# QKV product of tiles 6 to 15 as seven products of halves, second LayerNorm by algebra, W1 cast at the end of the stage

## The chip, the cores and the metric

One Trainium2 chip, one of its cores. The time is device microseconds of one execution, and lower is better. The kernel before takes 1277.43 us, the median of three runs (1275.66 to 1277.49). A profiled execution stands beside them; all shares and durations below are from it. Engines: PE (TensorE, products), ACT (ScalarE), DVE (VectorE), POOL (GpSimd), SP (which issues most DMAs).

## The reference

x has 2048 tokens of 576 features. Three things are added up, all on a normalized x.

```python
xn = _layernorm(x)
# A: sliding, dilated attention, 32 heads of 18
qkv = xn @ wqkv                                  # 576 x 1728
# each token sees itself and 7 earlier ones, 2 apart
a = softmax(q . k * 18**-0.5) . v @ wo
# B: a mixer
h = gelu(_layernorm(xn) @ w1)                    # 576 x 576
hs = shift_by_quarters(h) @ w2                   # +1, -1, +2, -2 tokens
x1 = xn + hs
b = x1 + gelu(_layernorm(x1) @ w3) @ w4          # 576 x 4608 x 576
out = x + a + b
```

The change touches `qkv = xn @ wqkv` and what is made beside it: xn, `_layernorm(xn)` and W1's cast.

## The kernel before, in words

Everything is float32, but products run on operands rounded to `fp32r`. To keep precision each operand is split into a rounded part "hi" (a cast on ACT) and the rest "lo" (a subtraction on DVE), and hi x hi, hi x lo and lo x hi are added up. With 576 = 4 x 128 + 64 features that makes 14 matmuls for one block of output, listed in `PAIRS`; the odd 64 features stand once as hi and once as lo in one slot.

A tile is 128 tokens; there are 16, and Y keeps all of them in SBUF. The order of the work on each engine is that of the Python code (`manual_schedule`): each engine and the DMA queue of SP take their instructions strictly in that order, and wait at semaphores. The stages are: QKV (to 194.9 us), the mixer with W1 and W2, the first part of the MLP plainly (with attention on DVE in between), the rest of the MLP by products of halves (`HALVES`, seven matmuls for a block of 288 features), and Wo.

The QKV stage, on which the change bears:

- `load_x`, `stats` and `norm_x` bring a tile, take its mean and variance (two BN_STATS, one aggregate, one addition on DVE, a power on POOL) and normalize it into Y. A second `stats(Y, 1, t)` takes them again for the second LayerNorm.
- `prep_x` (`transposes`, L137 to L149) turns a tile on PE (four transposes of 128 x 128 and every second tile a fifth for two tiles' odd features), casts hi on ACT (L142, L145) and takes lo on DVE (L146, L149).
- wqkv comes in five groups of columns (`COLS`: three of 288, two of 432) and is split once into WQ by `split_cg`.
- Tiles 0 to 3 take each group of columns as it comes (`q_cg`, L314, 14 matmuls, a copy L317 out of PSUM, a spill to DRAM). Tiles 4 to 15 take two halves of 864 columns each (`q_half` with `mm_tok`, L215: 28 matmuls of 432 columns, one copy L324, one spill).
- Beside them, tiles 0 to 15 are normalized again on DVE (`z_turn`), turned in 32 x 32 blocks (L161, L162) and put into DRAM, from where the mixer reads them by feature (`get`, `split_x`).
- `split_w1` casts W1 beside tiles 5 and 6, early in the stage; its tiles have a place of their own.

Of the kernel before, what the change touches and what calls it, by code (L numbers as in the profile page):

```python
# [17 lines left out]
NT = S // 128  # L18
# [39 lines left out]
def fused_block(ctx, tc, x, wqkv, wo, w1, w2, w3, w4, out):  # L58
# [46 lines left out]
    ztail = {}  # L105

    def tail_half(t):
        if t % 2 == 0:
            ztail[t // 2] = qpool.tile([128, 128], F32, name="ztail", bufs=2)
        return ztail[t // 2][:, t % 2 * 64:t % 2 * 64 + 64]  # L110

    def pair_tail(src, xts, t):
        return (src, [(xts, (t % 4 - 1) * 128), (xts, (t % 4) * 128)]) if t % 2 else None

# [16 lines left out]

    def transposes(src, tail, xt, col):
        ps = psb.tile([128, 2, 512], F32, name="ps", tag="b")
        p0 = ps[:, 0, :].rearrange("p (k c) -> p k c", k=4)
        p1 = ps[:, 1, :128]
        for k in range(4):
            pe.transpose(p0[:, k, :], src[:, k * 128:(k + 1) * 128], ident)  # L137
        rows = tail[0].shape[1] if tail else 0
        if tail:
            pe.transpose(p1[:rows], tail[0], ident)  # L140
        c = slice(col, col + 128)
        act.copy(xt[:, 0:4, c], p0)  # L142
        for i in range(rows // 64):
            xtt, ct = tail[1][i]
            act.copy(xtt[0:64, 4, ct:ct + 128], p1[64 * i:64 * i + 64])  # L145
        dve.tensor_tensor(xt[:, 5:9, c], p0, xt[:, 0:4, c].bitcast(F32), op=ALU.subtract)  # L146
        for i in range(rows // 64):
            xtt, ct = tail[1][i]
            dve.tensor_tensor(xtt[64:128, 4, ct:ct + 128], p1[64 * i:64 * i + 64],  # L149
                              xtt[0:64, 4, ct:ct + 128].bitcast(F32), op=ALU.subtract)  # L150

# [64 lines left out]
    w1p = tc.tile_pool(name="w1p", bufs=1, side="right", reuse_waits="tile")  # L218
    w1pool = w1p.__enter__()
    W1 = w1pool.tile([128, 10, 512], F32R, name="W1")  # L220
    W1R = w1pool.tile([128, 5, 128], F32R, name="W1R")
    room(w1pool)

    def z_turn(t):
        z = w1pool.tile([128, D], F32, name="z", bufs=1)
        norm(z, Y[:, t, :], 1, t)
        turn(z, t % 4)

    qp = tc.tile_pool(name="qp", bufs=1, reuse_waits="tile")
    qpool = qp.__enter__()  # L230
    WQ = qpool.tile([128, 10, 3 * D], F32R, name="WQ")
    xtile = {}
    xring = {}
    CG = 432
    COLS = [(0, 288), (288, 288), (576, 288), (864, 432), (1296, 432)]

    def load_x(t):
        xtile[t] = qpool.tile([128, D], F32, name="xin", bufs=3)
        sp.dma_start(xtile[t], xf[t * 128:(t + 1) * 128, :])

    def norm_x(t):
        norm(Y[:, t, :], xtile[t], 0, t)
        if t >= 4:
            dve.tensor_copy(tail_half(t), Y[:, t, 512:])
# [6 lines left out]
    def prep_x(t):  # L251
        xt = ring_block(("q", t // 4))
        if t < 4:
            tail = (Y[:, t, 512:], [(xt, t * 128)])
        else:
            tail = pair_tail(ztail[t // 2], xt, t)
        transposes(Y[:, t, :], tail, xt, (t % 4) * 128)
# [3 lines left out]
    def load_cg(cg, pieces):  # L261
        c, n = COLS[cg]
        r = qraw[cg] = qpool.tile([128, 5, n], F32, name="raw", bufs=2)
        if pieces:
            main_rows(r[:, 0:2, :], wqkv, c, n, 0, 2)
            main_rows(r[:, 2:4, :], wqkv, c, n, 2, 4)
        else:
            main_rows(r[:, 0:4, :], wqkv, c, n)
        dup_tail(r[:, 4, :], wqkv, c, n)
# [4 lines left out]

    load_x(0)
    load_x(1)
    load_cg(0, True)
    load_x(2)
    load_cg(1, False)
    load_x(3)  # L280
# [1189 lines left out]
```

## Time and profile before

| | |
|---|---|
| runs | 1277.49, 1275.66, 1277.43 us |
| profiled execution | 1279.68 us, its span from the first to the last instruction 1277.8 us |
| granted PE clock over the span | 0.998 |
| 0 to 8 us | PE 6.55 busy, DVE 3.75, ACT 3.19 |
| 8 to 20 us | PE 10.43 busy, DVE 9.31, ACT 5.21 |
| 195 to 254 us (mixer, W1) | PE 59.00 busy, DVE 34.79, ACT 36.05 |
| DMA over the span | 223.25 MB in 203800 packets, mean 175 GB/s |
| qkvd<-stg, x24 | 432 KB each, 3.9 us from issue to landing |

A row of the timeline reads: start, duration of the merged rows, engine, line, operation, out<-in, shape, count, and in brackets the idle time ahead of it with its releaser. In a group row the count is followed by the busy time, the mean ns of one, and the idle time ahead.

### The profile page before, as it was taken

To read this page: it belongs to the slowest core of one execution; us is meant where nothing else is said; L and a number is where in the kernel's file an instruction comes from. 1 tells how busy PE (TensorE), PEld (TensorE's weight loads), DVE (VectorE), ACT (ScalarE), POOL (GpSimd) and SP (SyncE) were. 2 spreads that over 40 slices of the span, in tenths; PEclk is the share of its full clock that TensorE was granted. 3 is DMA by queue.
4 is the path that set the end of the run, shared out by engine and by line. 5 is a ranking of instruction groups with operands and counts; after the bars stand their busy time and mean duration, and the time that the engine had idled before them with its cause. 6 is when DMAs were issued, how large, how long until landed. Compare 5 with 4: busy or idle time off the path is not lost.

```text
span 1277.8 us, 19971 instructions
## 1 busy us (share of the span) xinstructions
PE 1261.6 (99%) x7510; PEld 1155.8 (90%) x7510; DVE 900.3 (70%) x1203; ACT 722.2 (57%) x1155; POOL 253.0 (20%) x366
## 2 busy tenths in 40 slices
PE   9999999999999999999999999999999999999999
PEld 8999998899889999999889999998889898898898
DVE  6455533777648999998649998989899884464341
ACT  3332225525645545455777777776667776677730
POOL 2011100021122121212122232232122222222200
PEclk9999999999999999999999999999999999999999
DMA  7646774346897977769669889888958769899982
GB/s 206 154 123 141 165 173 145 85 119 200 192 239 167 231 146 158 151 141 243 119 131 213 197 175 219 183 162 209 259 84 197 146 116 189 183 213 216 259 256 84
DMA packets 203800, 223.25 MB, mean 175 GB/s; under 512 B 79528, under 2 KB 139528, under 8 KB 203576
## 3 DMA queue, kind: packets, MB, share of 16 engines
q1 hardware_dynamic: 170952, 155.18, 42.6%
q0 software_dynamic: 32752, 66.80, 32.6%
q8 instruction: 59, 0.97, 0.3%
q14 instruction: 37, 0.30, 0.1%
HBM read 124.47 MB, written 107.87 MB: 182 GB/s over the span
## 4 chain that ended last, share of the span: by engine, by line
PE 63%; DMA 3%; ACT 2%; DVE 2%; issue 1%; SPq 0%; DVEq 0%; ACTq 0%
PE ps L868 30%; PE cc L1130 19%; PE p L832 10%; PE ps L215 4%; DMA w3st<-in_B_w_dram 1%; DMA xt<-xn 1%; DVE w3st L965 1%; DMA x1n<-td1T 0%; DVE xt L597 0%; SPq L1178 0%; DMA Y<-od 0%; PE p L1437 0%; ACT Y L873 0%; ACT xt L927 0%; DVE w3a L976 0%
## 5 line engine op out<-in xcount | busy, mean ns | idle before, releaser
L868 PEld LDWEIGHTS ps<-w,c 128*128 128x128 f32 x3456 | 475.2, 188 | 22.5 <-ACT Y L873 3.2
L868 PE MATMUL ps<-w,c 128*128 128x288 f32 x3456 | 486.1, 294 | 6.2 <-ACT Y L873 2.1
L874 POOL DMA_DIRECT2D yd<-Y x154 | 138.4, 902 | 394.5 <-ACT Y L873 323.9
L826 DVE TENSOR_TENSOR c<-Y,c 128x512 fp32r<-128x512 f32 x144 | 98.8, 687 | 88.9 <-ACT Y L815 87.4
L873 ACT COPY Y<-ps 128x576 f32<-128x576 f32 x154 | 98.1, 637 | 75.2 <-PE ps L868 61.7
L215 PE MATMUL ps<-WQ,xt 128*128 128x432 f32 x672 | 134.8, 360 | 0.0
L215 PEld LDWEIGHTS ps<-WQ,xt 128*128 128x128 f32 x672 | 125.6, 188 | 5.7
L1130 PE MATMUL cc<-xt,w3s 128*128 128x512 f32 (+1 forms) x504 | 128.4, 394 | 1.0 <-DVE Y L1140 1.0
L1130 PEld LDWEIGHTS cc<-xt,w3s 128*128 128x128 f32 (+1 forms) x504 | 92.6, 189 | 19.5 <-DVE Y L1140 1.4
L876 ACT COPY Y<-ps 128x576 f32<-128x576 f32 x92 | 59.0, 641 | 65.6 <-PE ps L868 64.2
L1130 PE MATMUL cc<-x1n,w3a 128*128 128x512 f32 (+1 forms) x336 | 87.2, 399 | 1.4 <-ACT cc L1333 1.4
L746 DVE TENSOR_TENSOR po<-q,k 128x1152 f32<-128x1152 f32 (+1 forms) x48 | 84.3, 1756 | 0.8
L749 DVE TENSOR_REDUCE L<-po 128x64 f32<-128x1152 f32 (+1 forms) x48 | 84.1, 1751 | 0.8
L122 POOL TENSOR_TENSOR rs<-rs,mhalf 128x1 f32<-128x1 f32 x48 | 30.9, 645 | 260.1 <-DVE rs L121 147.7
L324 ACT COPY stg<-ps 128x864 f32<-128x864 f32 x24 | 21.2, 882 | 102.7 <-PE ps L215 60.4
L814 ACT ACTIVATE c<-p 128x512 fp32r<-128x512 f32 x48 | 28.7, 599 | 85.7 <-PE p L832 85.7
L722 DVE TENSOR_TENSOR po<-v,L 128x1152 f32<-128x1152 f32 x56 | 75.4, 1354 | 0.9
L1140 DVE TENSOR_TENSOR Y<-cc,Y 128x512 f32<-128x512 f32 x49 | 33.7, 688 | 59.9 <-ACT Y L1136 55.1
L1130 PEld LDWEIGHTS cc<-x1n,w3a 128*128 128x128 f32 (+1 forms) x336 | 61.1, 190 | 13.1 <-ACT cc L1333 1.9
L726 DVE TENSOR_TENSOR po<-po 128x1152 f32<-128x1152 f32 x49 | 66.4, 1355 | 0.9
L849 ACT COPY ps<-Y 128x576 f32<-128x576 f32 x92 | 59.4, 645 | 4.4 <-DVE Y L879 2.4
L215 PE MATMUL ps<-W,h 128*128 128x288 f32 x384 | 53.5, 295 | 0.0
(192 smaller groups left out, 1954.5 us busy)
## 6 DMA issues: line engine op xcount, KB each, us to landing
yd<-Y POOLq DMA_DIRECT2D x156, 288.0 KB, 5.8
Y<-in_B_w_dram SPq DMA_DIRECT2D x29, 576.0 KB, 5.8
w3st<-in_B_w_dram SPq DMA_DIRECT2D x56, 256.0 KB, 7.7
qkvd<-stg SPq DMA_DIRECT2D x24, 432.0 KB, 3.9
yd<-ev POOLq DMA_DIRECT2D x26, 288.0 KB, 7.0
w3st<-in_B_w_dram SPq DMA_DIRECT2D x92, 64.0 KB, 7.4
xd<-st SPq DMA_DIRECT2D x16, 320.0 KB, 6.0
xd<-big SPq DMA_DIRECT2D x16, 320.0 KB, 5.5
```

What stands on the lines that cost most here:

```text
L215: pe.matmul(ps[:, h, :n], xs(a), ws(b, h), start=i == 0, stop=i == len(PAIRS) - 1)
L722: dve.tensor_tensor(dst, vv, Lf[:, :, w:w + 1].to_broadcast([128, TPP * GH, HD]), op=ALU.mult)
L726: dve.tensor_tensor(o, o, dst, op=ALU.add)
L746: dve.tensor_tensor(dst, qf[:, None, :].to_broadcast([128, n, TPP * GC]), win, op=ALU.mult)
L749: dve.tensor_reduce(Lw[:, w:w + n, :], dst.rearrange("p w (x d) -> p w x d", d=HD), axis=AX.X, op=ALU.add)
L826: dve.tensor_tensor(h[:, 1, :], g, h[:, 0, :].bitcast(F32), op=ALU.subtract)
L832: pe.matmul(ps, W3[f][:, w, :], x1n[b][:, a, :], start=n == 0, stop=n == len(PAIRS) - 1)
L849: act.copy(ps[:, :, :HF], halves(t))
L868: pe.matmul(ps[:, k, :HF], h[:, col], w[:, p, k * HF:(k + 1) * HF], start=n == 0 and not seed, stop=n == len(seq) - 1, skip_group_check=True)
L873: act.copy(e.rearrange("p (h c) -> p h c", h=2), ps[:, :, :HF])
L874: pool.dma_start(yd[t], e, accum_op=ALU.add)
L1130: pe.matmul(ps, WX[w][:k, v, SLOT[w], :], area[sb][xk][:k, a, :], start=onto is None and i == 0, stop=last and i == len(HALVES) - 1, skip_ ...
```

## The change

The features are cut into two halves of 288 (two slots of 128 and one of 32, which holds hi and lo of the odd 32 features at different rows: `HALVES` then has seven matmuls for one half, `PLAIN` has 14 for both). wqkv is cut into six groups of 288 columns; three blocks b hold the groups b and b + 3.

Tiles 0 to 5 are multiplied plainly, in 36 units of 14 matmuls, `q_plain` (L363): tiles 0 to 3 for the groups 0, 3, 1, 4, 2, 5, then tiles 4 and 5 for 3, 4, 5, 0, 1, 2. PSUM has two banks for them, where `q_cg` had three pairs.

Tiles 6 to 15 go in five pairs p. For a pair and a block, tiles x halves of features are a 2 x 2 matrix A, halves of features x groups a 2 x 2 matrix B, and the product's four parts come from seven products of halves for eight (`step`, `seven`, L504). The sums of B (`sums_b`, on DVE, in the raw weights) and of A (`prep_lower`, `prep_upper`) are S1 = A21 + A22, S2 = S1 - A11, S3 = A11 - A21, S4 = A12 - S2 and T1 = B12 - B11, T2 = B22 - T1, T3 = B22 - B12, T4 = B21 with T2 taken off. A11 x B11 is copied into a second bank (L525), which A12 x B21 then adds to; S2 x T2, S3 x T3 and A22 x T4 add onto the first in turn, and what is needed on the way is kept by copies on ACT (L531, L537) and added on DVE (L515). A pair's three blocks g are 21 slots of seven matmuls, with two products of a block put behind the next block's first ones. The next pair is prepared in slots 5 to 14, four tiles' z in slots 7, 11, 15 and 17.

Each tile now takes six transposes: four of 128 features, and two of the odd 32 of each half, which ACT first copies four times side by side ("tails", L286) into a staging tile.

The second LayerNorm takes no statistics: xn has mean 0 and variance v r r (r = (v + 1e-5)^-0.5), so its factor is worked out from the first's numbers, for two tiles at a time (POOL, and one addition on DVE). z is then a scaling on ACT (L467), not a normalization on DVE.

W1 has no place until the last blocks: tiles 0 to 4 of Y go to DRAM (`away`), W1 is loaded into their place, cast in the slots 12, 13, 15, 17 and 18 of the last pair (`split_w1`), and Y is read back.

```diff
-    def transposes(src, tail, xt, col):
...
-        for k in range(4):
-            pe.transpose(p0[:, k, :], src[:, k * 128:(k + 1) * 128], ident)
...
+    def turned(t, ps):
+        y = Y[:, t, :]
+        tails = stage_tile()[:, 0:256]
+        act.copy(tails.rearrange("p (k r c) -> p k r c", k=2, r=4),
+                 y.rearrange("p (k c) -> p k c", k=2)[:, :, None, 256:]
+                 .to_broadcast([128, 2, 4, 32]))
+        for k in range(2):
+            for m in range(2):
+                c = k * HF + 128 * m
+                pe.transpose(ps[:, k, 128 * (m + 1):128 * (m + 2)], y[:, c:c + 128], ident)
+        for k in range(2):
+            pe.transpose(ps[:, k, 0:128], tails[:, 128 * k:128 * (k + 1)], ident)
...
+    def norm_x(t):
+        norm(Y[:, t, :], Y[:, t, :], 0, t)
+        if t % 2:
+            two = slice(t - 1, t + 1)
+            r = RS[1][:, two, 0:1]
+            pool.tensor_tensor(r, RS[0][:, two, 1:2], RS[0][:, two, 1:2], op=ALU.mult)
+            pool.tensor_tensor(r, r, MV[0][:, two, 1:2], op=ALU.mult)
+            dve.tensor_scalar(r, r, 1e-5, None, op0=ALU.add)
+            for k in (t - 1, t):
+                pool.tensor_tensor(RS[1][:, k, 1:2], RS[1][:, k, 0:1], mhalf, op=ALU.pow)
...
+    def q_plain(t, cg, mid=None):
+        ps = psa.tile([128, 512], F32, name="p1", tag="a")
+        xo, o = plain_x(t)
+        W, w = WB[cg % 3], OP["B12"] if cg > 2 else OP["B11"]
+        for i, (k, a, v) in enumerate(PLAIN):
+            if mid and i == 7:
+                mid()
...
+    mids = {1: lambda: prep_x(2), 2: lambda: prep_x(3), 19: lambda: prep_x(4),
+            20: lambda: prep_x(5), 28: lambda: lower(3), 30: lambda: upper(3)}
...
+            14: ((split_cg, 2),), 15: ((split_t, 1, False), (load_x, 7)),
+            16: ((stats_x, 5),), 17: ((norm_x, 5), (load_x, 8)), 18: ((split_cg, 5),),
+            20: ((sums_b, 2, 0), (load_x, 9)), 21: ((sums_b, 2, 1),), 22: ((stats_x, 6),),
+            23: ((stats_x, 7),), 24: ((norm_x, 7),), 25: ((norm_x, 6),),
+            26: ((split_t, 0, True),), 27: ((split_t, 2, False),), 29: ((split_t, 1, True),),
...
+            plan = {0: ((norm_x, 2 * n + 1),), 1: ((norm_x, 2 * n),), 5: ((low2, n),),
+                    9: ((up2, n),), 10: ((lambda n=n: cast_upper(n, two[n]),),),
+                    12: ((cast_s, n, 0),), 13: ((cast_s, n, 1),), 14: ((cast_s, n, 2),)}
+            for k, t in zip((7, 11, 15, 17), range(4 * (p - 3), 4 * (p - 3) + 4)):
+                plan[k] = plan.get(k, ()) + ((z_turn, t),)
+            if n < 7:
+                plan[2] = ((load_x, 2 * n + 3), (load_x, 2 * n + 2))
+                plan[18] = ((stats_x, 2 * n + 3),)
+                plan[19] = ((stats_x, 2 * n + 2),)
...
+            plan = {5: ((lambda: get(("z", 0), ring_block(("z", 0))),),),
+                    12: ((open_w1,), (split_w1, 0)), 13: ((split_w1, 1),),
+                    14: ((lambda: split_x(xring["z", 0], 0),),),
+                    15: ((split_w1, 2),), 16: ((lambda: split_x(xring["z", 0], 1),),),
+                    17: ((split_w1, 3),), 18: ((split_w1, 4),)}
...
+            order = ((g, 1), (g, 5), (g - 1, 4), (g, 6), (g - 1, 3), (g, 2), (g, 7))
+            if g == NGQ - 1:
+                order = ((g, 1), (g - 1, 4), (g, 5), (g, 6), (g - 1, 3), (g, 7), (g, 2),
+                         (g, 4), (g, 3))
```

Where instructions stand now, at three places. First ACT's queue where tile 4 is turned. Before: WQ and raw are the weights, ps the products' and the transposes' PSUM, xt the turned x.

```order
L317 COPY stg_565<-ps_550 128x432
L200 CAST WQ_118<-raw_414 128x3x432
L317 COPY stg_585<-ps_570 128x432
L200 CAST WQ_118<-raw_414 128x2x432
L142 CAST xt_590<-ps_591 128x4x128
L317 COPY stg_620<-ps_605 128x432
```

In the changed kernel, in units 18 and 19 (wb2 are the weights of block 2, p1 a unit's product, stg_729 the tails that PE turns in the middle of unit 19's product p1_720):

```order
L366 COPY stg_711<-p1_696 128x288
L247 CAST wb2_117<-rawb_485 128x576 x2
L255 CAST wb2_117<-rawb_485 96x2x288
L286 COPY stg_729<-Y_71 128x256
L297 CAST xt_737<-ps_728 128x2x256
L298 CAST xt_737<-ps_728 96x2x128
L366 COPY stg_749<-p1_720 128x288
```

Before, nothing that PE's transposes read came from ACT; now the tails copy stands behind a product's copy and three casts of weights.

Second, DVE's queue from the last two z of pair 3 to the first slot of pair 4 (ca1_1330 is the bank that A22 x T4 of the old block adds onto two slots later):

```order
L128 STREAM_TRANSPOSE st_1153<-z_1352 128x16x32
L129 STREAM_TRANSPOSE st_1153<-z_1352 128x4x32
L128 STREAM_TRANSPOSE st_1153<-z_1378 128x16x32
L129 STREAM_TRANSPOSE st_1153<-z_1378 128x4x32
L515 TENSOR_TENSOR keep_1288<-cc0_1162,keep_1288 128x288
L109 BN_STATS bn_82<-Y_71 128x6 x2
L110 BN_AGGR mv0_76<-bn_82 128x2
L111 TENSOR_SCALAR rs0_79<-mv0_76 128x1
L109 BN_STATS bn_82<-Y_71 128x6 x2
L110 BN_AGGR mv0_76<-bn_82 128x2
L111 TENSOR_SCALAR rs0_79<-mv0_76 128x1
L515 TENSOR_TENSOR keep_1343<-ca1_1330,keep_1343 128x288
```

Before, no sum on DVE freed a bank for PE in this stage; now the last row does, and two tiles' statistics and two turned z stand ahead of it.

Third, ACT's queue at the end of the stage. Before (xt_1573 is z's first block, h the mixer's first results):

```order
L324 COPY stg_1741<-ps_1712 128x864
L181 CAST xt_1573<-xt_1573 64x512
L182 CAST xt_1573<-xt_1573 64x512
L187 CAST xt_1573<-xt_1573 128x1024 x2
L324 COPY stg_1780<-ps_1751 128x864
L324 COPY stg_1812<-ps_1783 128x864
L324 COPY stg_1844<-ps_1815 128x864
```

In the changed kernel (xt_2313 is z's first block; cb, ca and cc are banks of the last two blocks, the copies out of them what PE waits for):

```order
L525 COPY cb1_2409<-ca1_2408 128x288
L148 CAST xt_2313<-xt_2313 64x512
L149 CAST xt_2313<-xt_2313 64x512
L154 CAST xt_2313<-xt_2313 128x1024
L513 COPY stg_2430<-ca0_2325 128x288
L167 CAST W1_2387<-Y_71 128x512
L167 CAST W1R_2388<-Y_71 128x4x16
L531 COPY keep_2439<-cc1_2438 128x288
L154 CAST xt_2313<-xt_2313 128x1024
L537 COPY keep_2457<-ca1_2408 128x288
```

W1's casts, which stood beside tiles 5 and 6, now stand between the copies of the last two blocks.

More of the change, by code (lines that the diff above doesn't have):

```diff
@@ L410, in fused_block @@
[L410 to L432 removed]
+    load_cg(1, raw_rows(10))
```

464 lines of the change are left out of this document (279 added, 185 removed).

## The prediction

> **What bounds the kernel now.** I read the page's engine shares first, then the windows by stage, then the timeline of the stage that the change rewrites.
>
> ```profile
> PE 1261.6 (99%) x7510; PEld 1155.8 (90%) x7510; DVE 900.3 (70%) x1203; ACT 722.2 (57%) x1155; POOL 253.0 (20%) x366
> ```
> ```profile
> 20.00:195.00 175.00, 175.00 (x953) 167.66 (x952) 88.91 (x229) 48.29 (x84) 18.54 (x28) 1.00 0.66 154
> ```
>
> The second row is the QKV stage (columns: PE, PEld, DVE, ACT, POOL busy, then the granted clock, here 1.00). PE has no idle time in it, DVE is busy for half of it and ACT for 28%. So the stage ends when TensorE has done its work, and each us of work taken away, or of waiting put in, moves the end of the program by as much. What comes behind the stage starts with the same products in both kernels; I carry the stage's difference to the end unchanged.
>
> Busy durations of a pipelined matmul say nothing of its price; distances between starts do. From the timeline of PE:
>
> ```profile
> 179.74 15.32 PE L215 MATMUL ps<-WQ,xt 128*128 128x432 f32 x77
> 194.90 9.71 PE L467 MATMUL ps<-xt,W 128*128 128x512 f32 x42
> ...
> 241.29 12.91 PE L467 MATMUL ps<-xt,W 128*128 128x512 f32 x56
> 254.04 3.33 PE L215 MATMUL ps<-W,h 128*128 128x288 f32 x24
> ...
> 257.75 3.35 PE L215 MATMUL ps<-W,h 128*128 128x288 f32 x24
> ```
> ```profile
> 43.22 0.60 PE L137 MATMUL ps<-ident,Y 128*128 128x128 f32 x4
> 43.57 8.45 PE L314 MATMUL ps<-WQ,xt 128*128 128x432 f32 x42
> 51.86 0.60 PE L137 MATMUL ps<-ident,Y 128*128 128x128 f32 x4
> ...
> 52.32 5.66 PE L314 MATMUL ps<-WQ,xt 128*128 128x432 f32 x28
> ```
>
> 77 products of 432 columns take 194.90 - 179.74 = 15.16: 0.197 each. 28 of 288 columns (24, and 4 not shown) take 257.75 - 254.04 = 3.71: 0.1325 each. Four transposes take 0.35 and a fifth 0.11 more.
>
> **Products and transposes.** I count from 20.0 us, where before has done tiles 0 to 3 for the first 288 columns. From there before has 112 products of 288 and 784 of 432: 14.8 + 154.4 = 169.2. The changed kernel has 32 plain units of 14 and 15 column blocks of 49, all of 288 columns: 448 + 735 = 1183 at 0.1325 = 156.7. That is **-12.5**. An eighth of ten tiles' work would be 13.8; narrower products cost 0.5% more per column, which takes back the rest. Transposes: before has twelve tiles left, six at 0.35 and six at 0.46 = 4.9; the changed kernel needs six for every tile, 12 x 0.57 = 6.8: **+2.0**. Without waits the stage would be 10.5 shorter.
>
> **The waits.** ScalarE and VectorE work strictly in order, and the changed kernel puts into ScalarE's queue a copy (the "tails" copy, L286) that TensorE waits for in the middle of its work. These rows price it:
>
> ```profile
> 13.79 0.27 PE L140 MATMUL ps<-ident,Y 128*64 128x128 f32 x1
> 14.74 1.72 PE L314 MATMUL ps<-WQ,xt 128*128 128x288 f32 x11 [0.28 <-ACT xt L142]
> ```
> ```profile
> 6.86 0.77 ACT L200 CAST WQ<-raw 128x288 fp32r<-128x288 f32 x2 [0.33 <-DMA raw<-in_A_wqkv_dram]
> ...
> 14.10 0.59 ACT L142 CAST xt<-ps 128x512 fp32r<-128x512 f32 x1 [2.74 <-PE ps L140]
> ...
> 18.06 0.40 ACT L317 COPY stg<-ps 128x288 f32<-128x288 f32 x1
> 18.35 1.50 ACT L200 CAST WQ<-raw 128x864 fp32r<-128x864 f32 x2
> 20.20 0.40 ACT L317 COPY stg<-ps 128x288 f32<-128x288 f32 x1 [0.35 <-PE ps L314]
> ```
> ```profile
> L200 ACT CAST W<-raw 128x512 fp32r<-128x512 f32 x5 | 3.1, 625 | 0.0
> L200 ACT CAST WQ<-raw 128x576 fp32r<-128x576 f32 x2 | 1.4, 680 | 0.0
> L200 ACT CAST W1R<-raw 128x64 fp32r<-128x64 f32 x5 | 1.2, 249 | 0.0
> L187 ACT CAST xt<-xt 128x1024 fp32r<-128x1024 f32 x8 | 8.3, 1048 | 0.0
> ```
>
> ScalarE starts 0.04 after a transpose's end (13.79 + 0.27, then 14.10), TensorE 0.05 after ScalarE's (14.10 + 0.59, then 14.74). A product of 288 ends about 0.16 after its successor could start, so a copy starts 0.20 after E, the moment at which the next group could issue. An independent successor starts 0.10 before the end of the instruction ahead (18.06, then 18.35 for a copy of 0.40).
>
> *The start.* Before ends its fourth unit at 20.20 - 0.20 = 20.0. In the changed kernel TensorE's first product stands behind tile 1's tails copy, and ScalarE's queue ahead of that copy is: two casts of W ending at 7.54 (the raw pieces arrive as now: 6.86 + 0.68), tile 0's tails (0.40), its casts (0.59, 0.40), W's tail cast (0.68). That puts the first product at 10.3, later than now; but of the waits that before has behind it (the 0.28 in the row of 14.74 is one) only two stay, for the normalized rows of tiles 2 and 3, and by the same rows the fourth unit ends at 20.0 again, its eight more transposes included. I take **0**, with 1.5 to either side.
>
> *Casts of W ahead of a tails copy*, three times (units 19, 28 and 30). After the unit before: copy at E + 0.20, three casts of 576 columns from E + 0.50 at 0.58 each, the tails copy (priced as a 288-column copy) from 2.24 to 2.64; TensorE goes on at 2.69. It had work, seven products and four transposes, until 0.93 + 0.44 = 1.37. That is 1.3 of waiting, 1.5 in unit 28, where two sets of casts follow each other: **+4.2**. The order of the queue fixes this; I allow 0.6 each way.
>
> *The tails copy in the column blocks*, two for each of the four pairs prepared there: a leaving product's copy at E + 0.20, the tails copy 0.50 to 0.90, TensorE at 0.95, its four transposes done at 0.44: 0.52, with the restart 0.55. Eight make **+4.4** (3.2, if all the copies are 0.15 shorter, to 7.2 if ScalarE is 0.35 behind each time).
>
> *The start of a pair's first block.* A22 x T4 of the old block adds onto the bank that VectorE reads after S3 x T3 two slots earlier. VectorE's queue there holds two turned z quarters and two tiles' statistics:
>
> ```profile
> L972 ACT ACTIVATE w3s<-w3st,kv 96x512 fp32r<-96x512 f32 x23 | 16.6, 720 | 0.0
> ```
> ```profile
> 28.32 0.81 DVE L119 BATCH_NORM_STATS2 bn<-Y 128x6 f32<-128x288 f32 x2
> ...
> 29.48 0.81 DVE L119 BATCH_NORM_STATS2 bn<-Y 128x6 f32<-128x288 f32 x2
> ```
> ```profile
> L161 DVE STREAM_TRANSPOSE st<-z 128x512 f32<-128x512 f32 x16 | 11.4, 712 | 6.0 <-DMA xd<-st 5.5
> L188 DVE TENSOR_TENSOR xt<-xt 128x1024 fp32r<-128x1024 f32 x8 | 9.7, 1220 | 3.6 <-ACT xt L187 3.5
> L162 DVE STREAM_TRANSPOSE st<-z 128x128 f32<-128x128 f32 x16 | 4.3, 270 | 0.0
> L201 DVE TENSOR_TENSOR W<-raw,W 128x512 fp32r<-128x512 f32 x5 | 3.4, 688 | 0.0
> L201 DVE TENSOR_TENSOR WQ<-raw,WQ 128x288 fp32r<-128x288 f32 x5 | 2.0, 455 | 0.0
> L201 DVE TENSOR_TENSOR W1R<-raw,W1R 128x64 fp32r<-128x64 f32 x5 | 1.1, 220 | 0.0
> ```
>
> From E of the slot with the last z: copy 0.20 to 0.50, z 0.78 (0.72 for 512 columns with a scale per row) to 1.28, transposes to 2.1, a sum to 2.5, two statistics at 29.48 - 28.32 = 1.16 to 4.8, the sum that is waited for to 5.25. TensorE is there after five products of seven, 4.64. 0.65, and 0.10 for the restart of the product pipe, at three pairs (the fourth prepares no statistics): **+2.2**, from 0 to 4.4.
>
> *W1's casts in the end.* In the last two column blocks (from the slot of A12 x B21 of the last but one, T = 0; a product group is 0.93) ScalarE gets W1's ten casts and z's four (5 x (0.625 + 0.249) + 2 x 0.625 + 2 x 1.05 = 7.7, or 6.3 with their overlaps) among the seven copies that TensorE waits for (2.1). VectorE gets eight long and five short subtractions (0.69 or 1.22, and 0.22).
>
> | product | without waits | waits for | ready | starts |
> |---|---|---|---|---|
> | A22 x T4 (last but one) | 2.8 | VectorE's sum behind W1's first subtractions | 3.3 | 3.4 |
> | S3 x T3 (last) | 7.1 | ScalarE's copy behind z's and W1's casts | 7.9 | 8.0 |
> | A22 x T4 (last) | 9.9 | VectorE's sum behind W1's last subtractions | 11.0 | 11.1 |
>
> 0.6 + 0.9 + 1.2 with restarts: **+2.8**, from 0 to 5. z's first block comes early enough not to matter:
>
> ```profile
> xt<-xd SPq DMA_DIRECT2D x6, 512.0 KB, 7.2
> ```
>
> It is asked for in slot 5, some 10 us ahead of its cast. After the stage only z's second block comes about 1 us later than before; three banks of the first mixing products cover that, and without the cover it costs that 1 us.
>
> **Sum.** -12.5 + 2.0 + 0 + 4.2 + 4.4 + 2.2 + 2.8 = **+3.1** against the profiled execution: 1279.68 (span 1277.8 and 1.9 around it) becomes 1282.8. The median of the runs is 1277.43, 2.25 less: **1280.5**. A measurement of this kernel tells about 0.2%, 2.6 us, from no change.
>
> **Rivals.**
>
> *The helpers keep up (not slower).* If VectorE and ScalarE are in time at the pairs' starts and in the end, 5.0 of waits go: 1275.5. It needs the chain of 5.25 shorter by 0.6, and the last two blocks' queues by 15%. For it: VectorE and ScalarE are half idle in the windows row, and the pairs' preparation is spread over 21 slots. Against it: the price is a burst's, not an average's.
>
> *The clock falls.* From the timeline and the windows later in before:
>
> ```profile
> 639.95 1.32 PE L868 MATMUL ps<-w,c 128*128 128x288 f32 x8 [1.39 <-DVE c L826]
> 641.58 3.05 PE L1130 MATMUL cc<-x1n,w3a 128*128 128x512 f32 x7 [0.31 <-ACT cc L1333]
> 644.43 2.22 PE L1130 MATMUL cc<-xt,w3s 128*128 128x512 f32 x7
> 646.49 1.75 PE L868 MATMUL ps<-w,c 128*128 128x288 f32 x12
> 648.08 1.79 PE L1130 MATMUL cc<-xt,w3s 128*128 128x512 f32 x7
> 649.70 1.75 PE L868 MATMUL ps<-w,c 128*128 128x288 f32 x12
> ```
> ```profile
> 636.00:644.00 8.00, 5.44 (x22) 3.94 (x21) 5.71 (x9) 6.67 (x11) 1.64 (x2) 0.87 0.39 47
> 644.00:652.00 8.00, 8.00 (x44) 7.05 (x43) 1.65 (x2) 4.02 (x7) 1.67 (x2) 0.91 0.75 185
> ```
>
> After two waits of 1.39 and 0.31 close together the granted clock falls below 1.00, and two groups of seven take 2.85 and 2.06, where one takes 649.70 - 648.08 = 1.62 later: 1.7 us lost. A wait of 1.5 (unit 28), with 1.3 in unit 30 behind it, or the two in the end, come near that; two falls make 1284. By the Trainium skill, page TensorE: Matmul & The Clock Gate, section A second HAM failure mode: psum-queue depth-cycling, frequent short idling between groups of matmuls lets the clock swing to half. By that rule the many waits here would bring falls, and the time would be this rival's; the trace agrees for the one place above.
>
> *Landings.* Every wait above takes the data as landed. Four spills of 144 KB per block go through SP's queue with z's, x's and W1's transfers; if a spill lands over 9 us late, its staging tile, and with it ScalarE and TensorE, wait. At 1 us in half of the 15 blocks: 1288.
>
> *The sevens don't run at 0.1325.* The second MLP's sevens take 1.62 / 7 = 0.231 each for 512 columns, against (254.04 - 241.29) / 56 = 0.228 in the first mixing products; 0.0037 more for 735 products is 2.7: 1283.
>
> **How the numbers follow.** Forecast 0.44, its own range 1278 to 1284; helpers keep up 0.27 (1272 to 1278); clock 0.10, landings 0.11, sevens 0.08. The range is 1272 to 1288: with every term at its low end the sum is 1272, with every term at its high end 1293, and the landings' worst lies above; what it leaves out is mostly there. Faster by over 0.2% (below 1274.9): 0.16, all from the helpers. Same: 0.11 from them and 0.17 of the forecast, 0.28. Slower: 0.27 of the forecast and the last three, 0.56.
>
> **What would show it.** In the changed profile: PE idle before L294 of about 1.3 us three times and 0.5 us eight times, released by ScalarE's L286; PE idle at L504 released by VectorE's L515 at three pair starts and twice in the end, and once by ScalarE's L537; starts of 288-column products in L504 at 0.1325; the first mixing product (L638) at about 198, not 194.90; clock 1.00 to there. I am wrong if waits at L294 sum to under 5 us, or if the stage ends before 194.

## The result, and the profile after

The changed kernel takes 1292.66 us, the median of four runs (1291.73 to 1293.49), beside 1277.46 for the kernel before (four runs, 1275.66 to 1279.24): a ratio of 1.0119, with a 95% interval of 1.0101 to 1.0136. It is slower, as forecast, but by 15.2 us and not by 3.1, and it lies above the range that ended at 1288. The profiled executions are 12.2 apart in their spans (1290.0 and 1277.8); the other 3 us come from which executions were profiled, since the one of before lies 2.2 above its median and the one of the changed kernel 0.9 below its own.

The page's engine row, and the windows row that answers to the stage of before, where TensorE had no idle time:

```profile
PE 1257.8 (98%) x7819; PEld 1155.1 (90%) x7819; DVE 933.3 (72%) x1219; ACT 773.2 (60%) x1297; POOL 255.2 (20%) x382
```
```profile
20.00:195.00 175.00, 164.44 (x1206) 158.69 (x1205) 114.06 (x230) 91.83 (x209) 18.64 (x37) 1.00 0.63 149
```

TensorE is busy for 3.8 us less in all, but idle for 10.6 of these 175. The list of waits on TensorE up to 209 us says on whom (total, times, longest; L392, the warm-up, is left out as it is the same before):

```profile
PE ps L294 <- ACT stg L286: 6.5, 5, 1.4
PE ca L504 <- DVE keep L515: 5.2, 13, 1.1
PE pp L294 <- ACT stg L286: 2.5, 7, 0.4
PE ca L504 <- ACT keep L537: 1.9, 1, 1.9
...
PE ps L292 <- DVE Y L119: 1.1, 1, 1.1
PE ps L292 <- DVE rs L220: 0.9, 1, 0.9
PE pp L292 <- DVE Y L119: 0.7, 1, 0.7
```

Five of these seven were in the forecast in some form. The 1.1 stands ahead of the first turn, which comes at 6.70 where before had it at 6.62, so it costs nothing; the 0.7 is a normalization in the first column block, which was not forecast. The surprise is the count in the second line: thirteen waits for VectorE's sum, where I had named three pair starts and two in the end. TensorE's timeline at the third slots of the first two blocks after pair 3's first, and in between a tails copy:

```profile
97.25 1.09 PE L504 MATMUL cc<-wb,xt 128*128 128x288 f32 x7
98.72 1.20 PE L504 MATMUL ca<-wb,xt 128*128 128x288 f32 x7 [0.38 <-DVE keep L515]
99.76 0.60 PE L292 MATMUL pp<-ident,Y 128*128 128x128 f32 x4
100.71 0.44 PE L294 MATMUL pp<-ident,stg 128*128 128x128 f32 x2 [0.35 <-ACT stg L286]
...
107.02 1.20 PE L504 MATMUL ca<-wb,xt 128*128 128x288 f32 x7 [0.30 <-DVE keep L515]
```

An idle time of 0.38 costs more than 0.38. Seven products of 0.133 from 97.25 end their issue at 98.18, so 98.72 is 0.54 late; and from 98.72 to 99.76 the next group takes 1.04 where 0.93 is plain. The wait costs 0.65. The waits are read from distances between starts in what follows, with 0.105 for such a restart.

VectorE is late for two reasons, one in the second and one in the third block of each of the pairs 3 to 6, and the trace has the same rows in all four. In the second block ScalarE and VectorE read the prepared tile's bank (pp) by turns, as in the timeline of all engines ahead of 98.72:

```profile
96.88 0.37 ACT L297 CAST xt<-pp 128x256 fp32r<-128x256 f32 x1 [0.81 <-DVE Y L322]
97.15 0.26 ACT L298 CAST xt<-pp 96x128 fp32r<-96x128 f32 x1
...
97.45 0.42 DVE L299 TENSOR_TENSOR xt<-pp,xt 128x256 fp32r<-128x256 f32 x1 [0.60 <-ACT xt L298]
...
97.88 0.29 DVE L301 TENSOR_TENSOR xt<-pp,xt 32x128 fp32r<-32x128 f32 x1
98.20 0.46 DVE L515 TENSOR_TENSOR keep<-ca,keep 128x288 f32<-128x288 f32 x1
```

VectorE had nothing to do for 0.60, and then its own sum stood behind two subtractions that had waited for ScalarE, which had waited 0.81 for VectorE. The product's bank was ready at about 97.4.

In the third block, ahead of 107.02, VectorE is simply busy. After one wait for ScalarE it goes without a gap through two subtractions, a sum, a turned z and a subtraction for the next pair's S (L340), while the bank was ready at about 105.8:

```profile
103.59 0.69 DVE L299 TENSOR_TENSOR xt<-pp,xt 128x512 fp32r<-128x512 f32 x1 [0.92 <-ACT xt L298]
...
106.52 0.45 DVE L515 TENSOR_TENSOR keep<-ca,keep 128x288 f32<-128x288 f32 x1
```

In the last pair, where no next pair is prepared, the same places in its first two blocks (185.04 and 191.55) have no wait.

The end of the stage, TensorE's timeline again, and the rows of SP (the read of z's first block) and ScalarE at the same place:

```profile
197.67 1.20 PE L504 MATMUL ca<-wb,xt 128*128 128x288 f32 x7 [0.39 <-DVE keep L515]
...
203.61 1.20 PE L504 MATMUL ca<-wb,xt 128*128 128x288 f32 x7 [1.94 <-ACT keep L537]
...
206.78 1.20 PE L504 MATMUL ca<-wb,xt 128*128 128x288 f32 x7 [1.05 <-DVE keep L515]
...
208.75 9.74 PE L638 MATMUL ps<-xt,W 128*128 128x512 f32 x42
```
```profile
193.59 1.10 SPq L141 DMA_DIRECT2D xt<-xd  x2
...
198.85 0.62 ACT L148 CAST xt<-xt 64x512 fp32r<-64x512 f32 x1 [1.10 <-DMA xt<-xd]
...
203.16 0.40 ACT L537 COPY keep<-ca 128x288 f32<-128x288 f32 x1
```

Mixing starts at 208.75: 13.85 later than before, and 10.7 later than the 198 that the forecast had. From there to the end the changed kernel is 1.65 shorter (1081.2 against 1082.9); over all traces that stretch takes 1079.9 to 1086.5, so nothing is read into it.

The start, TensorE's timeline, and two windows of 3.41 us (busy PE, PEld, DVE, ACT, POOL, then the granted clock):

```profile
8.73 0.44 PE L294 MATMUL ps<-ident,stg 128*128 128x128 f32 x2 [1.38 <-ACT stg L286]
...
10.99 0.69 PE L294 MATMUL ps<-ident,stg 128*128 128x128 f32 x2 [1.38 <-ACT stg L286]
11.33 4.41 PE L363 MATMUL p<-wb,xt 128*128 128x288 f32 x21
...
19.20 0.63 PE L292 MATMUL ps<-ident,Y 128*128 128x128 f32 x4 [0.94 <-DVE rs L220]
```
```profile
7.58:10.99 3.41, 0.88 (x7) 0.65 (x7) 2.47 (x6) 2.71 (x6) 1.81 (x3) 1.00 1.11 305
10.99:14.40 3.41, 3.41 (x15) 3.41 (x16) 3.23 (x8) 0.85 (x2) 0.55 (x1) 0.50 1.01 307
```

The first product starts at 11.33 (8.26 before, 10.3 forecast), and the clock is at half for the 3.41 us from 10.99 on. The 57th product, which begins the second group of columns, stands at 22.7, where before had it at 20.0.

### The profile page after: what moved, and what is told of

It reads as the page before. It is cut to its first block, busy times and chain, and to the rows that moved or that the text cites. A ratio compares the mean times of both kernels' runs of the same rounds, so it can differ in the third digit from the quotient of the medians.

```text
span 1290.0 us, 21004 instructions
## 1 busy us (share of the span) xinstructions
PE 1257.8 (98%) x7819; PEld 1155.1 (90%) x7819; DVE 933.3 (72%) x1219; ACT 773.2 (60%) x1297; POOL 255.2 (20%) x382
## 4 chain that ended last, share of the span: by engine, by line
PE 59%; DMA 5%; ACT 2%; DVE 2%; issue 1%; SPq 1%; DVEq 0%; ACTq 0%; POOLq 0%
PE ps L1039 28%; PE cc L1301 17%; PE p L1003 9%; PE ps L182 4%; DMA w3st<-in_B_w_dram 2%; DMA Y<-od 1%; SPq L1349 1%; DMA xt<-xn 1%; DMA xd<-big 0%; DVE w3st L1136 0%; DMA xt<-td0T 0%; DMA x1n<-td1T 0%; DVE xt L768 0%; ACT Y L1044 0%; PE p L1608 0%
## 5 line engine op out<-in xcount | busy, mean ns | idle before, releaser
L1039 PEld LDWEIGHTS ps<-w,c 128*128 128x128 f32 x3456 | 476.0, 188 | 23.2 <-ACT ev L1044 2.0
L363 PE MATMUL p<-wb,xt 128*128 128x288 f32 (+1 forms) x504 | 71.0, 301 | 0.0
L504 PE MATMUL ca<-wb,xt 128*128 128x288 f32 x420 | 63.9, 300 | 7.1 <-DVE keep L515 5.2
L363 PEld LDWEIGHTS p<-wb,xt 128*128 128x128 f32 (+1 forms) x504 | 69.0, 192 | 0.6 <-DVE wb L250 0.4
L504 PEld LDWEIGHTS ca<-wb,xt 128*128 128x128 f32 x420 | 57.4, 188 | 10.3 <-DVE keep L515 8.2
L112 POOL TENSOR_TENSOR rs<-rs,mhalf 128x1 f32<-128x1 f32 x32 | 19.4, 606 | 238.0 <-DVE rs L111 131.4
```

The source lines that it names most:

```text
L363: pe.matmul(ps[:, :QB], xo[:n, o + k, a, :], W[:n, w + k, v, :], start=i == 0, stop=i == len(PLAIN) - 1)
L504: pe.matmul(ps[:, :QB], xo[:n, XO[x], a, :], W[:n, OP[w], v, :], start=start and i == 0, stop=stop and i == len(HALVES) - 1, skip_group_ch ...
L1039: pe.matmul(ps[:, k, :HF], h[:, col], w[:, p, k * HF:(k + 1) * HF], start=n == 0 and not seed, stop=n == len(seq) - 1, skip_group_check=True)
```

## The experiments

The table gathers what the traces of the runs say: the start of the 57th product, of the first mixing product, the stage between them with 1.7 taken off where the clock fell inside it (the runs marked *; an estimate, half of 3.41 us), the median, and the mean granted clock of all runs of that kernel. The kernel before was run along with all of them: 23 runs, median 1276.89, mean clock 0.9989.

| kernel | 57th | mixing | between | median us | clock |
|---|---|---|---|---|---|
| before | 20.0 | 194.9 | 174.9 | 1276.89 | 0.9989 |
| changed | 22.7 | 208.75 | 186.05 | 1292.66 | 0.9965 |
| e1 tails early | 23.2 | 202.45 | 179.2 | 1286.5 | 0.9965 |
| e2 A22 x T4 later * | 21.3 | 203.9 | 180.9 | 1287.5 | 0.9955 |
| e3 filler * | 23.4 | 209.7 | 184.6 | 1293.3 | 0.998 |
| e4 end | 21.3 | 205.4 | 184.05 | 1288.2 | 0.9978 |
| e5 = e2, six buffers * | 21.7 | 202.2 | 178.8 | 1287.8 | 0.996 |
| e6 start * | 20.9 | 207.6 | 185.0 | 1292.0 | 0.9968 |
| c1 all but the start | 21.7 | 189.0 | 167.3 | 1277.0 | 0.9972 |
| c2 = c1 and start | 20.9 | 188.1 | 167.2 | 1274.8 | 0.9975 |
| d1 = c1, Y back later | 22.5 | 189.7 | 167.2 | 1274.8 | 0.9965 |
| c3 = c2, d1, two more | 21.9 | 188.15 | 166.3 | 1271.4 | 0.998 |
| b1 before, algebra | 20.6 | 196.9 | 176.3 | 1279.4 | 0.9989 |

My theory after the trace: the loss is helper waits, each set by an instruction's place in ScalarE's or VectorE's queue, and about a third of their time was not in the forecast. The rivals: the helpers are simply too full, so that a wait taken away comes back under another name; or the granted clock makes the loss.

### Tails copied a slot or a unit earlier

```diff
-            16: ((stats_x, 5),), 17: ((norm_x, 5), (load_x, 8)), 18: ((split_cg, 5),),
+            16: ((stats_x, 5),), 17: ((norm_x, 5), (load_x, 8)), 18: ((copy_tails, 4), (split_cg, 5)),
...
-            26: ((split_t, 0, True),), 27: ((split_t, 2, False),), 29: ((split_t, 1, True),),
+            26: ((split_t, 0, True),), 27: ((copy_tails, 7), (split_t, 2, False),), 29: ((copy_tails, 6), (split_t, 1, True),),
...
+            plan[8] = ((copy_tails, 2 * n),)
+            if n > 4:
+                plan[4] = ((copy_tails, 2 * n + 1),)
```

> ScalarE's tails copy is issued one slot or unit earlier: ahead of the casts of weights in units 18, 27 and 29, and in slots 4 and 8 of a pair in place of 5 and 9 (the first one of pair 3 stays, since its tile is not yet normalized). Nothing else moves. Theory (the copy's place in ScalarE's queue makes TensorE wait): the three waits in the units, 1.35 + 1.51 + 1.34 = 4.2 by the starts of the changed kernel's trace, and seven of 0.52 = 3.65 in the column blocks go, and with them the restarts behind them, about 10 x 0.055: -8.4 against 1292.7, so 1284.3. Rival (ScalarE is full at these places and the wait only changes its name, to a cast or a copy out of a bank): under 4 comes back, 1289 or more.

1286.5, a ratio of 1.0072 (1.0056 to 1.0087). The stage is 6.8 shorter. TensorE's waits from 24 us on:

```profile
PE ca L512 <- DVE keep L523: 5.1, 13, 1.0
PE ca L512 <- ACT keep L545: 2.1, 1, 2.1
PE p L371 <- ACT stg L374: 0.9, 1, 0.9
```

All waits for a tails copy are gone (the turns of tails are L302 in this kernel, and no line of the list has it; one more line, 0.6 for the normalization at the first block, is as it was). One new line, 0.9 for a product's copy in unit 29, is the rival's: with its restart it holds 1.1 of the 8.4 that were expected. The theory holds, with that exception.

### A22 x T4 one slot later, with five and with six buffers

```diff
-            order = ((g, 1), (g, 5), (g - 1, 4), (g, 6), (g - 1, 3), (g, 2), (g, 7))
+            order = ((g, 1), (g, 5), (g, 6), (g - 1, 4), (g - 1, 3), (g, 2), (g, 7))
```

> A22 x T4 of the old block stands one slot later in the next block (behind S2 x T2, where it stood ahead of it), so VectorE has three slots for the sum that frees its bank, where it had two. Theory (that sum is late in every block, not only at the pairs' starts): eleven waits go whose distances between starts are 0.49 to 0.79 in the changed kernel's trace, 6.96 in all where eleven plain distances are 1.46, so 5.5, and 11 x 0.10 of restarts: -6.6 against 1292.7, so 1286.1. My recorded step (only the three pair starts are late): -2.2, so 1290.5. Rival (a bank held one slot longer, or S4 x B22 directly behind it, waits in its place): 1292 or more.

1287.5, 1.0081 (1.0063 to 1.0100). TensorE's waits from 22 us on, and a row of ScalarE ahead of one of the tails copies:

```profile
PE pp L294 <- ACT stg L286: 4.0, 7, 1.8
...
PE ca L504 <- ACT keep L537: 3.0, 2, 2.7
...
PE ca L504 <- DVE keep L515: 0.2, 1, 0.2
```
```profile
165.50 0.40 ACT L537 COPY keep<-ca 128x288 f32<-128x288 f32 x1 [1.92 <-DMA qkvd<-keep]
```

The eleven waits for VectorE's sum are gone: the one of 0.2 left is in the end, where the order was not changed. So the sum was late in every block of pairs 3 to 6, and by less than a slot. The run does not tell the two reasons apart: it gives VectorE time whatever stands ahead of the sum. What the eleven gave was partly taken back by a buffer that a late spill still held (1.92, with TensorE waiting 1.84 behind it), a wait that had not been in the changed kernel at that place. The wait of the last block also grew, from 1.94 to 2.7; the clock fell there in this execution.

```diff
-            z5 = q2pool.tile([128, QB], F32, name="keep", bufs=5)
+            z5 = q2pool.tile([128, QB], F32, name="keep", bufs=6)
```

> As the run with A22 x T4 one slot later, and the buffers named keep are six where they were five. In that run ScalarE's copy of S2's bank waited 1.92 and 0.98 for a spill out of such a buffer (qkvd<-keep), and TensorE behind it 1.98 above a plain distance where 0.52 is the tails copy's. Theory (the spills hold the buffers, nothing else): those two waits go, about 1.5 and 0.5, so 1285.4 against 1287.5. Rival (the spills' queue is what is late, and a sixth buffer only puts the same wait off): 1287.

TensorE's wait at that place is 0.35 again, and the stage, its fall of the clock taken off, 2.1 shorter than with five buffers and 7.2 shorter than the changed kernel's. The median does not show it: 1287.8, 1.0089 (1.0069 to 1.0108), with the profiled execution at 1283.9 and the others up to 1290.5, at clocks from 0.999 to 0.994. The buffers are shown by the trace; by the time this run is inconclusive.

### Work for TensorE in the start

```diff
+        for i in range(filling.get(t, 0)):
+            pe.transpose(warm[:, :128], ident, ident)
...
-    for i in range(24):
+    for i in range(36):
```

> TensorE gets work that no result needs in the first 12 us: 36 turns of the identity in place of 24 ahead of tile 0, and 14 more each between the turns of tiles 0 and 1 and their tails. Theory (the granted clock falls from 10.99 to 14.41 us because TensorE idles 1.14, 1.38 and 1.38 us shortly before): the clock stays, and 14 products that stood 0.240 apart stand 0.133 apart: -1.5 against 1292.7, so 1291.2, and the first product still starts at 11.3. Rival (the clock falls for another reason, or the start waits for ScalarE and VectorE so that faster products only wait more): 1292.7.

1293.3, 1.0126 (1.0111 to 1.0141): nothing gained. The first row is the windows row of the start, whose clock stays at 1.00; the others, TensorE's timeline, show what took the place of slow products:

```profile
8.00:20.00 12.00, 10.30 (x84) 9.72 (x83) 8.81 (x20) 5.80 (x14) 3.54 (x7) 1.00 0.89 255
```
```profile
16.20 0.66 PE L294 MATMUL ps<-ident,Y 128*128 128x128 f32 x4 [0.86 <-DVE Y L119]
...
19.80 0.66 PE L294 MATMUL ps<-ident,Y 128*128 128x128 f32 x4 [0.84 <-DVE Y L119]
```

The added turns also held the first product back to 12.26. So the clock alone does not set the start: from the first product to the 57th it now takes 11.1 where the changed kernel takes 11.4, because TensorE then waits for VectorE to normalize tiles 2 and 3.

### The start's queues

```diff
+        copy_tails(k)
+    stats_x(2)
     prep_x(0)
     split_tail(qraw[0], 0, OP["B11"])
-    stats_x(2)
+    norm_x(2)
     prep_x(1)
```

> Only the start differs from the changed kernel. x's third tile is loaded ahead of the second group of weights; both first tails are copied ahead of tile 0's casts; VectorE takes tile 2's statistics ahead of tile 0's lo, and normalizes tile 2 ahead of tile 1's lo. Theory (the start waits in VectorE's and ScalarE's queues: tile 1's tails stand behind a cast of weights, tiles 2 and 3 are normalized behind three subtractions): the first product starts at about 8.8 where four executions so far had 10.1 to 11.7, and the fourth unit ends near 18.8 where they had 21.3 to 23.2; 1290.2 against 1292.7. Rival (the weights' landing or the clock sets the start): no change, 1292.7, with the fourth unit's end above 21.

The first product starts at 8.74, as expected, but the 57th at 20.9 and not at 18.8, and the time, 1.0112 (1.0097 to 1.0128), cannot be told from the changed kernel's. TensorE's waits up to 22 us:

```profile
PE p L371 <- DVE xt L307: 1.1, 1, 1.1
PE ps L300 <- DVE rs L220: 0.9, 1, 0.9
PE p L371 <- DVE wb L256: 0.4, 1, 0.4
```

All three are waits for VectorE and none is for ScalarE: what is moved ahead in VectorE's queue makes the next thing late. Executions with the start unchanged had the 57th product anywhere from 21.3 to 23.2, so 0.4 to 2.3 us are won at that point, and in the time nothing that can be measured.

### The end's casts elsewhere

```diff
-                    14: ((lambda: split_x(xring["z", 0], 0),),),
-                    15: ((split_w1, 2),), 16: ((lambda: split_x(xring["z", 0], 1),),),
-                    17: ((split_w1, 3),), 18: ((split_w1, 4),)}
+                    14: ((split_w1, 2),),
+                    15: ((lambda: split_x(xring["z", 0], 0),),), 17: ((split_w1, 3),),
+                    19: ((lambda: split_x(xring["z", 0], 1),), (split_w1, 4))}
```

> In the last pair the casts stand elsewhere: W1's third part in slot 14, z0's first in 15, W1's fourth in 17, z0's second and W1's fifth in 19. So nothing of z0 stands ahead of ScalarE's copies until it has landed, and only one cast group stands between A12's and S2's copies and the products that wait. Theory (the 1.94 and 1.05 at the end are ScalarE's and VectorE's queues, with z0's late landing in them): of 2.10 and 1.22 above a plain distance about 2.5 goes, 1290.2, and the wait at 203.61 is below 0.9. Rival (the casts are work that ScalarE or VectorE can't get done in the last two blocks wherever they stand): the waits move to the first mixing products or to the last sum, 1292 or more.

1288.2, 1.0088 (1.0073 to 1.0103), and the stage 2.0 shorter. The waits in the end:

```profile
PE ca L504 <- ACT keep L537: 0.9, 1, 0.9
PE ca L504 <- DVE keep L515: 0.2, 1, 0.2
```

1.1 in place of 3.4. They did not move to the mixing products. The theory holds in the main: the larger wait is 0.94, where less than 0.9 was expected. z's and W1's casts were moved together, so the run does not tell which of them held TensorE up. The time fell by more than the stage, by 4.5; in this execution the 57th product, whose code is unchanged, came 1.4 earlier.

### All of it together

c1 has the edits of e1 and e5, the end's casts behind the copies as in e4 (with z0's first cast in two parts, and the last block in another order), and T1, T3 and the statistics of tiles 8 and 9 in other units; c2 adds the start of e6.

```diff
+            26: ((split_t, 2, False),), 27: ((copy_tails, 7),), 28: ((stats_x, 9), (stats_x, 8)), 29: ((copy_tails, 6),),
...
+            32: ((cast_s, 3, 1),), 33: ((cast_s, 3, 2), (split_t, 1, True)), 34: ((norm_x, 9),),
+            35: ((split_t, 2, True),)}
...
+                    14: ((split_w1, 2), (split_w1, 3)), 15: ((split_w1, 4),),
...
-                order = ((g, 1), (g - 1, 4), (g, 5), (g, 6), (g - 1, 3), (g, 7), (g, 2),
+                order = ((g, 1), (g, 5), (g, 6), (g - 1, 4), (g - 1, 3), (g, 7), (g, 2),
```

> All that waited in the trace, except the start: tails copied one slot or unit earlier (for all tiles), A22 x T4 one slot later with six buffers, the end's casts behind the copies and S3 x T3 two slots behind S2 x T2 in the last block, and the sums T1 and T3 of weights spread so that the copy behind them (0.9 of waiting in the run with early tails) is free; tile 9's statistics taken earlier (0.8 of waiting at the first block). Theory (the waits are the loss, and each goes on its own): -8.2 for tails, -6.6 for VectorE's sums, -3.7 in the end, -0.8 for the norm: 1273.4, faster than the kernel before. Rival (ScalarE and VectorE are so tight that half of it comes back elsewhere): 1283, slower than before.

> The same with the start of the run e6_start. If the two add up, 2.5 less: 1270.9. If the start is set by landings, the same as without: 1273.4.

c1: 1277.0, 0.9997 (0.9985 to 1.0008). The stage went as expected, 18.8 shorter (19.3 forecast); the time did not, at 1277.0 where 1273.4 was expected. TensorE's waits from 22 to 260 us, and ScalarE just after the stage:

```profile
PE ps L664 <- DVE xt L155: 0.9, 1, 0.9
PE ps L649 <- DVE xt L155: 0.7, 1, 0.7
PE ca L512 <- ACT cb L533: 0.7, 1, 0.7
```
```profile
198.16 0.60 ACT L655 ACTIVATE g<-ps 128x512 f32<-128x512 f32 x1 [5.19 <-DMA qkvd<-keep]
```

Two of the three waits are new and lie in the mixer, whose first 250 products take 59.63 (56.87 before): a spill landed late, behind the reads that bring Y back. c2 is 1274.8, 0.9983 (0.9973 to 0.9992), 2.2 less than c1 where 2.5 was expected; 1270.9 had been its own figure.

```diff
         split_w(rem[:, :, 0:16], rem[:, :, 16:32], src[:, :, 128:144])
+
+    def back(k):
         sp.dma_start(Y[:, k, :], ysp[k])
...
+            if (b, i) in BACK:
+                back(BACK.index((b, i)))
```

> As c1, but the five reads that bring Y back from DRAM are issued among the first mixing products (after the third product group of its first block, and so on) instead of between the last spills of the stage. In c1 the mixer's first 250 products took 59.63 where the kernel before took 56.87: ScalarE waited 5.19 for a spill (qkvd<-keep) that landed late, and TensorE 0.69 and 0.94 behind it. Theory (1.4 MB of reads ahead of the last spills make them late): those 2.7 come back, 1274.3 against 1277.0. Rival (the spills are late by their own number, or the reads then delay W2): 1277.

1274.8, 0.9983 (0.9971 to 0.9994): 2.3 came back where 2.7 was expected. The mixer's first 250 products take 57.37.

```diff
-            1: ((norm_x, 3), (load_x, 4)),
+            1: ((load_x, 4),),
...
+    stats_x(3)
     prep_x(1)
...
-    split_tail(qraw[0], 0, OP["B11"])
+    split_tail(qraw[0], 0, OP["B11"], pool)
...
+            32: ((cast_s, 3, 1),), 33: ((cast_s, 3, 2), (split_t, 1, True)), 34: ((split_t, 2, True),),
+            35: ((norm_x, 9),)}
```

> As c2, with three things more: Y read back later as in d1 (-2.7), the last split of weights a unit earlier, so that the first block's copy into the second bank is not behind it (0.68 of waiting, with its restart -0.9), and in the start tile 3's statistics ahead of tile 1's lo and one subtraction of weights on GpSimd (the fourth unit's end from 20.9 to about 19.6, -1.3). Theory (they add up): 1274.8 - 4.9 = 1269.9. Rival (the granted clock, which averaged 0.997 over c1's and c2's runs and 0.9986 over those of before, takes part of it, some 1.7 for each fall): 1272 or more.

1271.4, 0.9954 (0.9939 to 0.9968): 5.5 faster than the kernel before and 21.3 faster than the changed one; the expectation was 1269.9. Its windows row over the stage:

```profile
23.00:188.00 165.00, 164.98 (x1248) 164.32 (x1248) 118.71 (x242) 96.29 (x224) 17.84 (x38) 1.00 0.71 169
```

No wait is left there, with ScalarE and VectorE as busy as in the changed kernel. That settles it against the rival of full helpers: but for one subtraction of the start, which GpSimd now does, their work is all there, in other places. The clock as the whole cause falls too: d1 ran 17.9 shorter than the changed kernel at the same mean clock, 0.9965. The start did not follow: the 57th product is at 21.9, with a fall of the clock from 13.20 on, where 19.6 was expected.

### The algebra alone, in the kernel before

```diff
-        norm(z, Y[:, t, :], 1, t)
+        act.activation(z, Y[:, t, :], AF.Identity, scale=RS[1][:, t, 1:2])
...
-        stats(Y[:, t, :], 1, t)
```

> The kernel before with only the second LayerNorm's factor by algebra, and z as a scaling on ScalarE. VectorE loses 16 statistics and 16 normalizations, some 16 x (1.16 + 0.58) = 28 us of its 900, ScalarE gets 16 x 0.78. Theory (TensorE has no idle time in the stage of before, so VectorE's time there is worth nothing): 1277.1, within 0.2%. Rival (the additions that wait for GpSimd stand in VectorE's queue in the start, ahead of the split of weights): 1 to 2 slower.

1279.4, 1.0017 (1.0008 to 1.0027): slower, by some 2 us. The line of TensorE's waits up to 200 us that grew most, first of before, then of this kernel:

```profile
PE ps L137 <- DVE Y L129: 0.5, 2, 0.4
```
```profile
PE ps L137 <- DVE Y L129: 1.6, 6, 0.4
```

VectorE has 25 us less to do (875.0 against 900.3) and is later: its turned z now waits for ScalarE (13 times up to 200 us, 25.1 in all), and the next tile's normalization stands behind it. Neither theory had that. My rival's place was another, the start, where 0.6 of it is.

## Why the prediction was right and wrong, step by step

The direction was right, and so were the products' usual spacing, the places and sizes of the tails waits, and the pair starts. The table gives each step against the changed kernel's trace, restarts counted in.

| step | forecast | measured |
|---|---|---|
| products and transposes | -10.5 | -8.6 (c3, without waits, against before: 166.3 and 174.9) |
| the start | 0 | +2.7 |
| casts ahead of a tails copy, three | +4.2 | +4.4 |
| tails copies in the blocks | +4.4 | +4.0 for seven; at the first +0.8 for the normalization |
| the sum, at the three pair starts | +2.2 | +2.3 |
| the sum, at the eight other blocks | none | **+4.4** |
| the end | +2.8 | +4.2 |
| to the start of mixing | +3.1 | +13.85 (the rows add up to 14.2) |

- **The step that failed first** is that VectorE's sum would be late only where two turned z and two tiles' statistics stand ahead of it. It was late in all eleven blocks of pairs 3 to 6. I priced only the burst at a pair's start. In the second blocks a chain in which ScalarE and VectorE wait for each other over one prepared tile stands ahead of the sum, and in the third blocks a turned z and the next pair's subtractions do. e2 shows that all eleven waits end with one slot more; that these two are what makes VectorE late is read from the trace, and neither was taken away by itself.
- **The start** I set at 0 by letting two delays cancel. They did not: the first product came 1.0 later than my 10.3, and from there to the 57th it took 11.4 where I had 9.7, with the clock at half for 3.41 us and the wait for tile 3 that I had counted. e3 shows that the clock is not the only bound there, since without the fall waits for tiles 2 and 3 take nearly all of it back; e6 shows that moving work in VectorE's queue brings back only part. What would set the start right was not found.
- **The end** had the three products, in their order. Its size failed at S3 x T3, which cost 2.2 and not 0.9, and there at the sentence that z's first block comes early enough not to matter. The read stands in slot 5 (187.84), 9.9 ahead of the moment at which ScalarE was free for its cast, much as I had it; but SP's queue issued it only at 193.59, behind spills and the writes of z. It landed some 5.3 later, sooner than the 7.2 that I had, but 1.10 after ScalarE was ready for it, in front of the copy that TensorE needed. e4 took 2.0 back.
- **Products and transposes** were 1.9 too good. In c3's stage the products' plain distances average 0.1337 and not 0.1325 (1.4 in all; the usual one is 0.133, and eight of 0.19 to 0.27 add the rest). A set of six transposes costs 0.11 more than I took, since the second product behind it stands 0.217 behind the first (1.3 for twelve sets); but in the kernel before a set costs 0.09 more too, so only some 0.3 of that is in the difference.
- **The rivals.** The clock's came in beside the forecast, not in its place, and in the start, where I had not put it; the 25 waits from 22 us to the mixing products brought no fall, with a clock of 1.00 over that stretch. Over all runs the mean clock is 0.9965 against 0.9989; 0.0024 x 1277 is 3 us, some two falls. It is part of the 15.2, not the cause of it: e3, at a mean clock of 0.998, was as slow, and d1, at 0.9965, was 17.9 shorter. Landings came with e2 and c1, once other waits were gone. That the helpers keep up was wrong for this order, and right for c3's.
- **A step that I did not price**: the algebra. Alone it costs 2 us in the kernel before, which I would have called hidden. How much of the changed kernel's loss is its own was not tried.
- **The sums.** The range stopped at 1288, though I put the sum of all high ends at 1293; the ends given for each term add up to 1290 or 1291, and the measured 1292.7 lies above them, since the start went past its own bound of 1.5, the products had no bounds, and the eight ordinary blocks had no term at all. Narrower products cost 1% more per column by the distances shown (0.1325 for 288, 0.197 for 432), not 0.5%; the -12.5 does not use that figure. The end's three rows add up to 2.7, not 2.8.

## What to carry to other kernels

When a stage is bound by one engine and the others are half idle, ask of every copy and sum that the bound engine waits for what stands ahead of it in its own queue, in an ordinary step as well as in a burst; a mean load of half or two thirds says nothing on that. Issue such a helper a slot early, or let its consumer come a slot later, before judging the arithmetic: the same products went from 1.2% slower to 0.5% faster by order, one more buffer, and one subtraction moved to GpSimd. Ask the same of the DMA queue: a read that the program asks for early is only as early as the queue ahead of it lets it be. And count a chain in which two helpers read one bank by turns as one piece of work.

## What the runs showed of the hardware

*The granted clock changes in fixed windows.* In the thirteen traces every fall that ends within the program lasts 3.41 us, and the falls of one trace start a whole number of 3.4133 us apart (in d1 at 10.89, 328.33 and 635.53: 93 and 90 windows). Cutting each trace into these windows, all 16 inside the program with TensorE busy for less than 1.66 of 3.41 us are followed by a fall, none of those with more than 1.84 is, and between them 4 of 12 are: about half a window. One window at the very end of b1, busy for 1.6, has none behind it in the trace. Two rows of the kernel before and two of c1 show it at the same place in the program, the second row of each pair being the window after:

```profile
638.54:641.95 3.41, 1.72 (x11) 1.42 (x11) 2.54 (x4) 2.58 (x5) 0.61 (x1) 1.00 0.73 91
641.95:645.36 3.41, 3.41 (x10) 2.65 (x9) 0.69 (x1) 2.44 (x6) 0.17 (x1) 0.50 0.28 29
```
```profile
633.44:636.85 3.41, 1.99 (x12) 1.65 (x12) 2.78 (x5) 2.40 (x4) 0.64 (x1) 1.00 0.68 83
636.85:640.26 3.41, 3.10 (x15) 2.45 (x14) 1.23 (x2) 3.38 (x7) 0.78 (x1) 1.00 0.22 23
```

The same waits can fall into one window or across two, which would make one kernel's executions differ; there is one trace of each kernel, so this is read from times alone. Of c1's ten runs two were 1273.2 and 1274.0 at a clock of 1.0, and five 1276.3 to 1277.6 at 0.997, some 3.4 more: two falls of 1.7. By the Trainium skill, page TensorE: Matmul & The Clock Gate, section Part 1: The HAM clock gate (the "warmup" mystery), the window is 3413 ns and free-running, and the clock is gated after an idle window. The trace agrees on the window; it differs on idle, since windows with TensorE busy for up to 1.83 us were enough.

*A short wait costs more than the idle time shown*: 0.38 shown was 0.65 in all (at 98.72 in the changed kernel).
